# Retention of the first nine chunks in whole chunks of 128 tokens, the others in halves of 64 in quarters of the array

## The chip, the cores and the metric

The kernel runs on one core of one Trainium2 chip. The metric is the device time in microseconds (us) of one execution. Three runs of the kernel before gave 443.77, 444.45 and 444.71 us, a median of 444.45 us. A profile shows one further execution of it.

## The reference

Inputs are queries, keys and values of 4 batches, 8 heads, 768 tokens and 64 features, in float32. A retention layer with one decay per head is followed by a mixture of experts that sends each of the 3072 tokens to one of 8 experts (512 to 1024 to 512 features):

```python
gamma = 1.0 - 2.0 ** (-5.0 - np.arange(H, dtype=np.float32))
for t in range(S):
    state = gamma[None, :, None, None] * state + np.einsum('bhd,bhe->bhde', k[:, :, t], v[:, :, t])
    y[:, :, t] = scale * np.einsum('bhd,bhde->bhe', q[:, :, t], state)
...
logits = x @ w_gate + modality_bias[modality_id]
e_idx = np.argmax(logits, axis=1)
...
for e in range(E):
    mask = e_idx == e
    h = np.maximum(x[mask] @ w1[e], 0.0)
    out[mask] = gate_w[mask, None] * (h @ w2[e])
```

## The kernel before, in words

**Retention.** The 4 batches of 768 tokens are 24 chunks of 128 tokens (`NN`), six to a batch (`NCH`). The decay is taken out of the recurrence: values are scaled per token and head by a negative power of gamma on GpSimd (`decay_v`, tile `vd`), outputs by a positive power further on (`gain`). What is left for a chunk is plain matrix work in float32: scores (keys times queries, tile `sc`), a causal mask on VectorE (tile `a`), the output of a chunk (tile `y`), which is the state (tile `s`) times the queries plus the masked scores times the values, and the update of the state in PSUM (tile `st`), which ScalarE copies to SBUF (`keep_state`).

Each chunk is worked on in two halves of 64 tokens. All operands then are 64 by 64, and a matmul uses one quarter of the 128 by 128 array. `scores`, `grown` (state update) and `heads_out` (output) only make lists of matmuls; `run` issues two lists in turns of two matmuls, so that four quarters have work at once. The order within a chunk is written out in `quarters(n)`: the second half's state update and the scores of chunk n+1, in turns with the output of chunk n; then a `yield`; then the rest, with the first half's state update of chunk n+1.

**Tokens and routing.** `tokens_out` turns the output of the chunk before by a matmul with the identity and the gate's weights (tile `x`, line 308), so that it has features and logits of 128 tokens. After every third chunk `route` puts small steps on a list `todo`; the main loop takes one off at each `yield` (`tick`). They find each token's expert and its row in a DRAM tensor `x_dram` sorted by expert, and GpSimd scatters the rows there with indirect DMAs (line 414). After some groups (`EVENTS`), the first of them group 1 (chunks 3 to 5), a list of full slots of 256 rows is made: matmul `pt` (line 621), VectorE `lst` (line 625).

**Experts.** SyncE waits for that list, reads it into registers (line 879), and loads the rows (`xg`, line 735) and the weights (`raw`, lines 707 and 709). A first guess of the expert, after group 0, starts the weights earlier. Rows are transposed (`xp_e`, line 754), everything is split into a high and a low part in a reduced float32 format (ScalarE `hi`, line 713, VectorE `lo`, line 715), and the two layers are matmuls `h_e` (line 769) and `o_e` (line 784). The first job begins in the middle of chunk 9 (`DENSE`); from there on the steps of retention are put between the steps of the experts, in a fixed order. The last rows go through two static small units (`uh_u`, line 838) and a loop.

**Loads.** `load_kq` and `load_kv` put a chunk's keys and queries by feature, and its keys and values by token, on SyncE's DMA queue; SyncE works its queue off in order.

Of the kernel before, what the change touches and what calls it, by code (L numbers as in the profile page):

```python
# [7 lines left out]
F32 = mybir.dt.float32  # L8
# [26 lines left out]
NTAIL = 2  # L35
NUNIT = 144
DENSE = 9
EMPTY = 2 * NCAND
ZROW = NE * NT

# [3 lines left out]
FC = DF // P  # L44
QW = KC * 256

C_ID, C_MASK, C_DEC, C_IOTA, C_OUT, C_HALF, C_END = 0, 128, 256, 304, 312, 360, 424


@with_exitstack  # L50
def kernel(
# [23 lines left out]
    def bank(name):  # L75
        return ps.tile([P, 512], F32, tag="bank", name=name)
# [42 lines left out]

    gain = cst[:, C_OUT : C_OUT + NCH * H].rearrange("p (c h) -> p c h", h=H)  # L120
    half = cst[:, C_HALF : C_HALF + D]

    tbias = cp.tile([P, NN, NE], F32, name="tbias")
    iota3 = cp.tile([P, GRP, NE], F32, name="iota3")
# [81 lines left out]
    def masked(n):  # L206
        att[n] = wk.tile([P, 2, NG, D], F32, tag="a", name=f"a_{n}")
        nc.vector.tensor_tensor(
            att[n].rearrange("p u g t -> p (u g) t"),
            psc.pop(n).rearrange("p u g t -> p (u g) t"),  # L210
            half.unsqueeze(1).to_broadcast([P, H, D]), op=ALU.mult,
        )
# [51 lines left out]

    def quarters(n):
        more = 0 <= n and (n + 1) % NCH
        ys = []
        if n >= 0:  # L270
            py = bank(f"y_{n}").rearrange("p (g t) -> p g t", g=NG)
            ys = heads_out(n, py)
# [10 lines left out]
        if n >= 0:  # L283
            yield n
# [6 lines left out]
        if n < 0:  # L291
            return None
# [5 lines left out]
        nc.scalar.copy(yT, py)  # L298
        return yT
# [644 lines left out]

    def decay_v(n):
        vv = kvs[n][:, 1].rearrange("p (h e) -> p h e", h=H)
        vds[n] = wk.tile([P, H, D], F32, tag="vd", name=f"vd_{n}", bufs=3)
        ins = nc.gpsimd.tensor_tensor(  # L948
            vds[n], vv, dec[:, n % NCH].unsqueeze(2).to_broadcast([P, H, D]), op=ALU.mult
        )  # L950
        vd_last[:] = [getattr(ins, "ins", ins)]

# [169 lines left out]
def _layout(inputs):  # L1122
    import numpy as np

    f = np.float32
    q, k, v = inputs["q"], inputs["k"], inputs["v"]

    def feat(a):
        a = a.transpose(0, 1, 3, 2).reshape(B, NG, P, NCH, P)
        return a.transpose(0, 3, 2, 1, 4).reshape(NN, P, DM)  # L1130

    def toks(a):

        a = a.reshape(B, NG, 2, NCH, 2, D, D).transpose(0, 3, 2, 5, 4, 1, 6)
        return a.reshape(NN, P, DM)
# [7 lines left out]
    cst[:, C_DEC : C_DEC + NCH * H] = dec.reshape(P, NCH * H)  # L1143
    cst[:, C_IOTA : C_IOTA + NE] = np.arange(NE)
# [6 lines left out]
    cst[:, C_HALF:] = np.tile(np.triu(np.ones((D, D))), (2, 1))  # L1151
# [25 lines left out]
    return {n: np.ascontiguousarray(a) for n, a in arrs.items()}  # L1177
# [35 lines left out]
```

## Time and profile before

| | |
|---|---|
| median of three runs | 444.45 us (443.77 to 444.71) |
| profiled execution | 440.58 us |
| its span, first to last instruction | 438.5 us |
| TensorE (PE) busy | 402.6 us, 92% |
| VectorE (DVE) / ScalarE (ACT) / GpSimd (POOL) busy | 242.8 / 208.1 / 101.9 us |
| mean granted TensorE clock | 0.967 |
| first scores / first transposes of rows / first expert matmul | 5.26 / 64.02 / 67.38 us |

Times count from the start of the span. "PE" is matmuls, "PEld" their weight loads; a float32 matmul of the program is two instructions of each in the trace. Ends of matmuls are modelled, so the distance between starts says more than a length. A bracket behind a row gives the idle time of its engine ahead of it and what ended it; "issue" means that the engine waited for nothing the profile shows.

### The profile page before, as it was taken

Reading aid. Unit: us, or ns where it says so; the run is one execution under the profiler, and the core shown is the slowest. Engines: PE = TensorE matmul, PEld = TensorE weight load, DVE = VectorE, ACT = ScalarE, POOL = GpSimd, SP = SyncE. Lnnn points to the kernel's source line nnn. Section 1 sums busy time; section 2 is a strip of 40 time slices with the busy share of each in tenths; the row PEclk is TensorE's granted clock in tenths of the full one; section 3 lists DMA queues with packets and bytes.
Section 4 is the critical chain, followed back from the end, with each engine's and each line's share of the span. In section 5 each row is a group of like instructions: output and inputs, shape, how many; then the busy total and the mean of one; then the engine's idle time right before and its main releaser. Section 6 shows DMA issues by size and latency. Waiting matters only on the chain.

```text
span 438.5 us, 13128 instructions
## 1 busy us (share of the span) xinstructions
PE 402.6 (92%) x5156; PEld 352.2 (80%) x5156; DVE 242.8 (55%) x581; ACT 208.1 (47%) x419; POOL 101.9 (23%) x130
## 2 busy tenths in 40 slices
PE   3777788999999998999999999999999999999990
PEld 3766677878988987988888988989898898869850
DVE  1452738756656647745754765887565664635400
ACT  1331436636447555446445636645454646445310
POOL 2423312152132024021311131030486101001010
PEclk9885989999999999999999999999999999999996
DMA  8999639985967682345770224662253999995000
GB/s 287 384 386 301 218 118 305 357 271 207 323 209 243 230 314 90 116 162 178 245 277 25 76 77 165 217 194 73 92 175 117 338 343 356 332 400 222 2 24 20
DMA packets 30895, 92.83 MB, mean 212 GB/s; under 512 B 5550, under 2 KB 5678, under 8 KB 30832
## 3 DMA queue, kind: packets, MB, share of 16 engines
q1 hardware_dynamic: 25360, 77.83, 51.4%
q0 software_dynamic: 5184, 13.67, 8.3%
q8 instruction: 41, 0.67, 0.7%
q10 hardware_dynamic: 288, 0.48, 0.3%
q14 instruction: 22, 0.18, 0.1%
HBM read 94.81 MB, written 17.21 MB: 255 GB/s over the span
## 4 chain that ended last, share of the span: by engine, by line
PE 58%; issue 14%; DMA 3%; DVE 3%; ACT 2%; POOL 2%; SPq 1%; POOLq 0%; ACTq 0%
PE o_e L784 21%; PE h_e L769 21%; PE x L308 4%; PE h_s L769 3%; PE sc L263 3%; PE st L263 2%; PE y L263 2%; DVE lo_e L715 2%; DMA wa_u<-in_w_dram 2%; PE xp_e L754 1%; DMA kq<-in_qkv_dram 1%; ACT hi_e L713 1%; POOL out_dram L797 1%; DMA xg_e<-x_dram 1%; PE uh_u L838 0%
## 5 line engine op out<-in xcount | busy, mean ns | idle before, releaser
L715 DVE TENSOR_TENSOR lo_e<-raw,hi_e 128x1024 fp32r<-128x1024 f32 x80 | 99.3, 1241 | 70.1 <-ACT hi_e L713 64.9
L769 PE MATMUL h_e<-xTh,hi_e 128*128 128x256 f32 x320 | 92.2, 288 | 0.9 <-ACT hi_e L713 0.9
L769 PE MATMUL h_e<-xTh,lo_e 128*128 128x256 f32 x320 | 90.5, 283 | 0.9 <-DVE lo_e L715 0.9
L769 PE MATMUL h_e<-xTl,hi_e 128*128 128x256 f32 x320 | 90.5, 283 | 0.0
L713 ACT CAST hi_e<-raw 128x1024 fp32r<-128x1024 f32 x80 | 83.8, 1047 | 0.0
L784 PE MATMUL o_e<-hi_e,hTh 128*128 128x512 f32 x160 | 66.2, 414 | 0.0
L784 PE MATMUL o_e<-lo_e,hTh 128*128 128x512 f32 x160 | 63.3, 396 | 0.0
L784 PE MATMUL o_e<-hi_e,hTl 128*128 128x512 f32 x160 | 63.1, 394 | 0.0
L769 PEld LDWEIGHTS h_e<-xTh,hi_e 128*128 128x128 f32 x320 | 61.2, 191 | 1.9 <-ACT hi_e L713 1.1
L769 PEld LDWEIGHTS h_e<-xTh,lo_e 128*128 128x128 f32 x320 | 61.2, 191 | 1.4 <-DVE lo_e L715 1.1
L769 PEld LDWEIGHTS h_e<-xTl,hi_e 128*128 128x128 f32 x320 | 61.2, 191 | 0.0
L948 POOL TENSOR_TENSOR vd<-kv,cst 128x512 f32<-128x512 f32 x24 | 26.8, 1117 | 115.6 <-PE y L263 54.8
L722 ACT ACTIVATE hTh<-h_e 128x256 fp32r<-128x256 f32 x80 | 30.5, 387 | 35.3 <-PE h_e L769 30.0
L263 PE MATMUL sc<-kq 64*64 64x64 f32 x768 | 37.4, 239 | 9.0 <-DMA kq<-in_qkv_dram 5.3
L723 DVE SCALAR_TENSOR_TENSOR hTl<-h_e,hTh 128x256 fp32r<-128x256 f32 x80 | 33.2, 419 | 21.1 <-ACT hTh L722 19.8
L258 ACT COPY s<-st 128x256 f32<-128x256 f32 x44 | 16.5, 375 | 58.4 <-PE y L263 31.2
L797 POOL DMA_INDIRECT out_dram<-o_e,xg_e x20 | 20.7, 1035 | 92.1 <-ACT o_e L796 86.2
L263 PEld LDWEIGHTS sc<-kq 64*64 64x64 f32 x768 | 30.7, 149 | 11.0 <-DMA kq<-in_qkv_dram 5.3
L330 ACT ACTIVATE xs<-x,cst 128x64 f32<-128x64 f32 x96 | 22.2, 315 | 33.9 <-issue 24.6
L414 POOL DMA_INDIRECT x_dram<-xs,pos x24 | 25.6, 1067 | 49.2 <-DVE xs L380 22.2
L263 PE MATMUL st<-vd,kv 64*64 64x64 f32 x704 | 33.3, 240 | 3.2 <-ACT s L258 1.1
L784 PEld LDWEIGHTS o_e<-lo_e,hTh 128*128 128x128 f32 x160 | 30.1, 188 | 7.3 <-DVE lo_e L715 0.3
(181 smaller groups left out, 707.0 us busy)
## 6 DMA issues: line engine op xcount, KB each, us to landing
raw<-in_w_dram SPq DMA_DIRECT2D x104, 512.0 KB
kv<-in_qkv_dram SPq DMA_DIRECT2D x24, 512.0 KB
kq<-in_qkv_dram SPq DMA_DIRECT2D x23, 512.0 KB
xg_e<-x_dram SPq DMA_DIRECT2D x20, 257.0 KB
wa_u<-in_w_dram SPq DMA_DIRECT2D x8, 512.0 KB
wb_u<-in_w_dram SPq DMA_DIRECT2D x16, 256.0 KB
xg_s<-x_dram SPq DMA_DIRECT2D x4, 257.0 KB
x_dram<-xs,pos POOLq DMA_INDIRECT x24
```

What stands on the lines that cost most here:

```text
L263: nc.tensor.matmul(out_, l, r, start=start, stop=True, skip_group_check=True)
L308: nc.tensor.matmul(px[:, g], yT[:, 2 * u + g], wgt[:, 2 * u + g], start=(g == 0), stop=(g == 1), skip_group_check=True,)
L330: nc.scalar.activation(x[:, i], px[:, i // 2, rows(i % 2)], AF.Copy, scale=gain[:, c, 4 * u + i : 4 * u + i + 1],)
L414: ins = nc.gpsimd.indirect_dma_start(out=x_dram[:, :], out_offset=bass.IndirectOffsetOnAxis(ap=pos[:, i : i + 1], axis=0), in_=xs, in_offs ...
L713: nc.scalar.copy(hi, raws[m][i])
L715: nc.vector.tensor_tensor(lo, raws[m][i], hi.bitcast(F32), op=ALU.subtract)
L722: nc.scalar.activation(hi, src, AF.Relu)
L723: nc.vector.scalar_tensor_tensor(lo, src, 0.0, hi.bitcast(F32), op0=ALU.max, op1=ALU.subtract)
L769: nc.tensor.matmul(ph, s["w1"][f // 2][wi][:, o : o + P], s["xT"][kc // 2][a][:, kc % 2, :], start=(n == 0), stop=(n == 3 * KC - 1),)
L784: nc.tensor.matmul(po, hT[f][a][:, hh * P : (hh + 1) * P], s["w2"][f // 2][wi][:, (f % 2) * DM : (f % 2 + 1) * DM], start=(n == 0), stop=( ...
L797: ins = nc.gpsimd.indirect_dma_start(out=out[:, :], out_offset=bass.IndirectOffsetOnAxis(ap=xg.bitcast(I32)[:, DM : DM + 1], axis=0), in_= ...
L948: ins = nc.gpsimd.tensor_tensor(vds[n], vv, dec[:, n % NCH].unsqueeze(2).to_broadcast([P, H, D]), op=ALU.mult)
```

## The change

Chunks 0 to 8 (`WHOLE = 9`) are no longer halved. `whole_scores(n)` takes one head's 64 features by all 128 tokens: two heads at a time use the upper and lower half of the rows of the array, each into a PSUM bank of its own, and VectorE masks them in two operations of 512 columns where it had one. `whole_state(n)` contracts over all 128 tokens, two heads side by side in the columns, and `keep_state` copies the state once per chunk where it did twice. `whole_out(n)` does the state's part in quarters with 128 columns and the values' part over all 128 tokens. Chunks 9 to 23 keep `quarters`; `first_halves(9)` does ahead of them what the last `quarters` would have done. The masked scores of whole chunks live in the buffers of the cut weights `hi12` and `hi13`. The values' scales of whole chunks are 48 more columns of the constants, and the host lays out keys and values by token differently for these chunks.

```diff
+    def whole_scores(n):
+        kt, qt = feat(n, 0), feat(n, 1)
+        p = [bank(f"sc{j}_{n}").rearrange("p (g t) -> p g t", g=NG) for j in range(2)]
+        for g in range(NG):
+            for j in range(2):
+                nc.tensor.matmul(
+                    p[j][:, g], kt[rows(j), g], qt[rows(j), g], start=True, stop=True,
+                    skip_group_check=True,
+                )
+        att[n] = me.tile([P, 2, NG, P], F32, tag=f"hi1{2 + n % 2}", name=f"a_{n}")
+        for j in range(2):
+            nc.vector.tensor_tensor(
+                att[n][:, j], p[j], mask.unsqueeze(1).to_broadcast([P, NG, P]), op=ALU.mult
+            )
+
+    def whole_state(n):
...
+        for g in range(NG):
+            for j in range(2):
+                nc.tensor.matmul(
+                    p[rows(j), g], kk[:, 2 * g + j], vds[n][:, 2 * g + j],
+                    start=(c == 0 and g == 0), stop=True, skip_group_check=True,
+                )
+        keep_state(n + 1, 0)
...
+    def whole_out(n):
...
+                    nc.tensor.matmul(
+                        py[rows(1 - j), g], s[rows(j), g], qt[rows(j), g], start=(g == 0),
+                        stop=True, skip_group_check=True,
+                    )
+        for g in range(NG):
+            for j in range(2):
+                nc.tensor.matmul(
+                    py[rows(1 - j), g], vd[:, 2 * g + j], a[:, j, g],
+                    start=(s is None and g == 0), stop=True, skip_group_check=True,
+                )
+        yT = wk.tile([P, NG, P], F32, tag="yT", name=f"yT_{n}")
+        nc.scalar.copy(yT, py)
+        return yT
+
+    def first_halves(n):
+        run(scores(n))
+        run(grown(n, 0))
+        keep_state(n, 1)
+        masked(n)
...
     def retention(modi):
-        list(quarters(-1))
-        masked(0)
+        whole_scores(0)
...
         for n in range(NN):
-            yT = yield from quarters(n)
-            if n + 1 < NN:
-                masked(n + 1)
+            if n < WHOLE:
+                if (n + 1) % NCH:
+                    whole_state(n)
+
+                load_kv(n + 7 if n < 3 else n + 3)
+                if n + 1 < WHOLE:
+                    whole_scores(n + 1)
+                else:
+                    first_halves(n + 1)
+                yield n
+                if prev is not None:
+                    tokens_out(*prev)
+                    if n % GRP == 0:
+                        route(n // GRP - 1)
+                    prev = None
+                yT = whole_out(n)
+            else:
+                yT = yield from quarters(n)
+                if n + 1 < NN:
+                    masked(n + 1)
+                load_kv(n + 3)
             if n + 2 < NN:
                 decay_v(n + 2)
-
-            load_kv(n + 7 if n < 3 else n + 3)
             load_kq(n + 8 if n < 4 else n + 4)
```

TensorE, chunk 2, before (kq_117 are chunk 2's keys and queries, kq_125 chunk 3's; vd_250 is chunk 2's scaled values, vd_342 chunk 3's; s_2 are two copies of the state; the lines left out go on in the same turns):

```order
L308 MATMUL x_0_371<-wgt,yT_246 128x144 x2
L308 MATMUL x_1_376<-wgt,yT_246 128x144 x2
L263 MATMUL st_166<-vd_250,kv_119 64x64 x2
L263 MATMUL y_386<-kq_117,s_2_286 64x64 x2
...
L263 MATMUL sc_387<-kq_125 64x64 x2
L263 MATMUL y_386<-kq_117,s_2_336 64x64 x2
...
L263 MATMUL sc_387<-kq_125 64x64 x2
L263 MATMUL y_386<-a_340,vd_250 64x64 x2
...
L263 MATMUL st_166<-vd_342,kv_127 64x64 x2
L263 MATMUL y_386<-a_340,vd_250 64x64 x2
```

and with the change (vd_204 is chunk 2's scaled values there, and sc has two tiles):

```order
L293 MATMUL st_167<-vd_204,kv_119 64x64 x8
L275 MATMUL sc_3_318<-kq_125 128x128
L275 MATMUL sc_3_319<-kq_125 128x128
...
L366 MATMUL x_0_333<-wgt,yT_279 128x144 x2
L366 MATMUL x_1_338<-wgt,yT_279 128x144 x2
L307 MATMUL y_347<-kq_117,s_2_228 64x128 x8
L313 MATMUL y_347<-a_242,vd_204 64x128 x8
```

The turns of output with scores and state update are gone: state update, scores of the next chunk, tokens of the last, output follow each other, each in a shape of its own, with 32 matmuls in place of 64 beside the tokens' four.

SyncE's queue at the first list, before (lst_1018 is the list of group 1, xg_e_1053 the first rows; raw_109 is the last piece of the guessed weights):

```order
L707 DMA raw_109<-in_w_dram 128x1024
L102 DMA kq_618<-in_qkv_dram 128x1024
L879 TENSOR_LOAD lst_1018
L879 ISA x2
...
L735 DMA xg_e_1053<-x_dram 128x514
```

and with the change (lst_767 is that list, kv_747 are the keys and values by token of chunk 10):

```order
L765 DMA raw_109<-in_w_dram 128x1024
L104 DMA kq_474<-in_qkv_dram 128x1024
L110 DMA kv_747<-in_qkv_dram 128x1024
L937 TENSOR_LOAD lst_767
L937 ISA x2
...
L793 DMA xg_e_802<-x_dram 128x514
```

One load, that of chunk 10, has moved from behind the list to ahead of it.

More of the change, by code (lines that the diff above doesn't have):

```diff
@@ L37 @@
 DENSE = 9
+WHOLE = 9
 EMPTY = 2 * NCAND
@@ L45 @@
 QW = KC * 256
[L47 removed]
+C_ID, C_MASK, C_DEC, C_IOTA, C_OUT, C_HALF, C_DECW, C_END = 0, 128, 256, 304, 312, 360, 424, 472
 @with_exitstack
@@ L121 @@
     half = cst[:, C_HALF : C_HALF + D]
+    decw = cst[:, C_DECW : C_DECW + NCH * H].rearrange("p (c h) -> p c h", h=H)
     tbias = cp.tile([P, NN, NE], F32, name="tbias")
@@ L263, in run @@
                 nc.tensor.matmul(out_, l, r, start=start, stop=True, skip_group_check=True)
-    def quarters(n):
[L268 to L272, printed above, removed]
+    def whole_scores(n):
[12 more added lines that the diff above has]
+            )
@@ new lines, in whole_state @@
+    def whole_state(n):
+        c = n % NCH
+        if c == 0:
+            pst[n // NCH] = bank(f"st_{n}")[:, : NG * D].rearrange("p (g e) -> p g e", g=NG)
+        p = pst[n // NCH]
+        kk = kvs[n][:, 0].rearrange("p (h d) -> p h d", h=H)
+        for g in range(NG):
[5 more added lines that the diff above has]
+        keep_state(n + 1, 0)
+        if c == NCH - 2 and n + 1 < WHOLE:
+            pst.pop(n // NCH)
@@ new lines, in whole_out @@
+    def whole_out(n):
+        py = bank(f"y_{n}").rearrange("p (g t) -> p g t", g=NG)
+        qt, a, vd, s = feat(n, 1), att.pop(n), vds.pop(n), sts.pop((n, 0), None)
+        if s is not None:
+            for g in range(NG):
[4 more added lines that the diff above has]
+                    )
+        for g in range(NG):
+            for j in range(2):
+                nc.tensor.matmul(
[5 more added lines that the diff above has]
+        return yT
@@ L273, in quarters @@
+    def first_halves(n):
[3 more added lines that the diff above has]
+        masked(n)
+    def quarters(n):
+        more = (n + 1) % NCH
+        py = bank(f"y_{n}").rearrange("p (g t) -> p g t", g=NG)
+        ys = heads_out(n, py)
         own = grown(n, 1) if more else []
@@ L946, in decay_v @@
         vv = kvs[n][:, 1].rearrange("p (h e) -> p h e", h=H)
+        by = decw if n < WHOLE else dec
         vds[n] = wk.tile([P, H, D], F32, tag="vd", name=f"vd_{n}", bufs=3)
         ins = nc.gpsimd.tensor_tensor(
-            vds[n], vv, dec[:, n % NCH].unsqueeze(2).to_broadcast([P, H, D]), op=ALU.mult
+            vds[n], vv, by[:, n % NCH].unsqueeze(2).to_broadcast([P, H, D]), op=ALU.mult
         )
@@ L1130, in feat, with whole @@
         return a.transpose(0, 3, 2, 1, 4).reshape(NN, P, DM)
+    def whole(a):
+        return a.transpose(0, 2, 1, 3).reshape(NN, P, DM)[:WHOLE]
     def toks(a):
+        w = whole(a)
         a = a.reshape(B, NG, 2, NCH, 2, D, D).transpose(0, 3, 2, 5, 4, 1, 6)
-        return a.reshape(NN, P, DM)
+        return np.concatenate([w, a.reshape(NN, P, DM)[WHOLE:]])
     gam = 1.0 - 2.0 ** (-5.0 - np.arange(H, dtype=np.float64))
@@ L1143, in _layout @@
     cst[:, C_DEC : C_DEC + NCH * H] = dec.reshape(P, NCH * H)
+    dec = (gam[None, :] ** (-t[:, None])).reshape(NCH, P, H)
+    cst[:, C_DECW:] = dec.transpose(1, 0, 2).reshape(P, NCH * H)
     cst[:, C_IOTA : C_IOTA + NE] = np.arange(NE)
@@ L1150, in _layout @@
     cst[:, C_OUT : C_OUT + NCH * H] = gain.transpose(1, 0, 2).reshape(P, NCH * H)
-    cst[:, C_HALF:] = np.tile(np.triu(np.ones((D, D))), (2, 1))
+    cst[:, C_HALF : C_HALF + D] = np.tile(np.triu(np.ones((D, D))), (2, 1))
     ci = np.arange(NCAND)
```

5 lines of the change are left out of this document (1 added, 4 removed).

## The prediction

> **What bounds the kernel now.** I read the page first, then busy time by stretch, then the order of single instructions around the first list of rows.
>
> ```profile
> PE   3777788999999998999999999999999999999990
> PEclk9885989999999999999999999999999999999996
> ...
> 8.30:64.00 55.70, 43.92 (x1201) 39.10 (x1202) 24.84 (x109) 17.76 (x57) 17.24 (x30) 0.82 0.83 294
> 68.60:421.00 352.40, 347.37 (x3826) 305.18 (x3827) 213.77 (x466) 183.00 (x350) 80.31 (x91) 1.00 0.60 207
> ```
>
> The second pair gives, per stretch, its length, busy PE, PEld, DVE, ACT and POOL, granted clock, DMA share and GB/s. From 68.6 to 421 us TensorE is busy 347.37 of 352.40 us at full clock: the expert matmuls, in one fixed order. The change leaves that stretch alone, so the end moves by as much as its start moves. Before it lies a head of 55.70 us, in which the first nine chunks run by themselves; there PE idles 11.8 us and the clock averages 0.82. By stretch:
>
> ```profile
> 8.30:13.40 5.10, 4.62 (x128) 4.43 (x128) 1.01 (x5) 0.74 (x2) 3.05 (x11) 1.00 1.06 367
> 13.40:16.80 3.40, 1.56 (x82) 1.27 (x82) 2.02 (x10) 1.23 (x3) 0.55 (x2) 1.00 1.02 405
> 16.80:20.20 3.40, 3.40 (x73) 3.28 (x64) 1.72 (x10) 0.86 (x2) 1.89 (x2) 0.50 1.03 406
> 20.20:30.50 10.30, 6.88 (x248) 6.16 (x250) 5.02 (x23) 4.38 (x17) 1.38 (x6) 1.00 1.03 389
> 30.50:44.10 13.60, 11.34 (x268) 9.84 (x261) 4.32 (x20) 3.02 (x9) 5.25 (x6) 0.50 0.94 302
> 44.10:57.80 13.70, 9.92 (x292) 8.38 (x288) 8.17 (x39) 4.61 (x15) 5.13 (x6) 1.00 0.62 221
> 57.80:61.20 3.40, 3.40 (x57) 3.00 (x51) 1.59 (x6) 1.04 (x3) 0.00 (x0) 0.50 0.09 22
> ```
>
> and, as single instructions (start, length, instruction):
>
> ```profile
> 10.17 0.32 PE L263 MATMUL st<-vd,kv 64*64 64x64 f32 x2
> 10.18 0.32 PE L263 MATMUL y<-kq,s 64*64 64x64 f32 x2
> 10.27 0.32 PE L263 MATMUL st<-vd,kv 64*64 64x64 f32 x2
> ...
> 14.25 0.23 PE L263 MATMUL st<-vd,kv 64*64 64x64 f32 x2
> 14.26 0.23 PE L263 MATMUL y<-kq,s 64*64 64x64 f32 x2
> 14.31 0.23 PE L263 MATMUL st<-vd,kv 64*64 64x64 f32 x2
> ```
>
> Three stretches are at 0.50. The first one is too, though the profile gives it 1.00: four quarter instructions start every 0.10 us at 10.2 and every 0.06 us (0.058 over longer runs) at 14.3. The clock falls after a stretch that PE spent half idle (1.56 of 3.40 busy before 16.8) and rises after a full one. Half clock covers 4.62 + 3.40 + 11.34 + 3.40 = 22.8 us of busy time, so about 11.4 us are lost to it. The idle time has this form:
>
> ```profile
> 16.55 0.27 PE L263 MATMUL y<-kq,s 64*64 64x64 f32 x1 [1.37 <-issue]
> 34.22 0.37 PE L263 MATMUL y<-kq,s 64*64 64x64 f32 x2 [1.07 <-issue]
> ...
> q8 instruction: 41, 0.67, 0.7%
> ```
>
> PE waited for nothing the profile shows. PE ran 10,312 matmuls and loads; 0.67 MB for them is 64 bytes each, and 41 packets is 16 KB, 256 instructions, each. A chunk of quarters is 128 matmuls and 128 loads: one packet per chunk. I read those gaps as PE running out of instructions (a guess: the view only names them "issue").
>
> **The change, part by part.** Per chunk it replaces 64 quarter matmuls by 32 (each is two instructions in the trace), run two at a time in place of four. Prices:
>
> ```profile
> 379.77 1.93 PE L838 MATMUL uh_u<-wa_u,uxT_u 128*32 128x256 f32 x32
> 381.64 0.39 PE L769 MATMUL h_s<-xTh,hi_s 128*128 128x256 f32 x1
> 62.93 1.25 PE L308 MATMUL x<-wgt,yT 128*128 128x144 f32 x8
> 64.02 1.34 PE L754 MATMUL xp_e<-cst,xg_e 128*128 128x128 f32 x8
> 119.84 0.28 PE L769 MATMUL h_e<-xTh,lo_e 128*128 128x256 f32 x1
> 119.96 0.28 PE L769 MATMUL h_e<-xTl,hi_e 128*128 128x256 f32 x1
> 120.17 0.27 PE L263 MATMUL st<-vd,kv 64*64 64x64 f32 x2
> ```
>
> The tail unit runs four column tiles over all 128 rows: 32 instructions of 256 columns in 1.87 us, 0.058 us each. Each tile thus gets a new one every 0.23 us. Half the columns on half as many tiles at once give the same pitch, so a pair with 128 columns starts every 0.058 us, one with 64 columns every 0.029. So whole scores cost 16 x 0.058 = 0.93 us, the state's part of the output 0.93, the values' part 0.93, the state update 0.46: 3.25 us, against 128 x 0.058 / 4 = 1.86. The token matmuls (8 in 1.09 us, from 62.93 to 64.02) stay. Going from one shape of the array to another costs 0.09 us (119.96 to 120.17 is 0.21, where the pitch is 0.12); whole chunks do it four times, quarters twice. A chunk is thus 3.13 us before and 4.70 now, **1.6 us more at full clock**; over the head, 12 to 13 us more.
>
> The Trainium skill, TensorEngine Tiling (Array Packing), Tiling Modes, says that a change of tiling mode drains the array. By the trace that drain is 0.09 us; if it took a whole instruction, 0.27 us, the 18 extra changes would cost 3.2 us more, and the forecast below would be about 2 us faster than before instead of 5.
>
> What pays for it is time in which PE now does nothing or runs at half clock. I lay out the new order from 8.30 us, where the first state update starts as before (values scaled on POOL wait for the constants, which grow by a ninth). The rows that pin it:
>
> ```profile
> 7.21 1.04 POOL L948 TENSOR_TENSOR vd<-kv,cst 128x512 f32<-128x512 f32 x1 [6.12 <-DMA cst<-in_consts_dram]
> 44.89 2.23 PE L308 MATMUL x<-wgt,yT 128*128 128x144 f32 x16
> 45.06 0.59 ACT L298 COPY yT<-y 128x512 f32<-128x512 f32 x1
> 49.66 0.20 PE L548 MATMUL pc<-ones,crep 128*96 128x1 bf16 x1 [0.84 <-DVE crep L543]
> 51.18 0.40 PE L570 MATMUL pk<-dg,onef 96*96 96x96 f32 x2
> 54.09 0.21 PE L621 MATMUL pt<-ohs,vals 96*1 96x2 bf16 x3 [0.18 <-DVE ohs L611]
> 57.44 0.15 DVE L625 TENSOR_TENSOR lst<-pt,base_e 1x6 int32<-1x6 f32 x1 [3.40 <-remote]
> 60.03 1.67 SPq L735 DMA_DIRECT2D xg_e<-x_dram  x2
> L208 DVE TENSOR_TENSOR a<-sc,cst 128x512 f32<-128x512 f32 x9 | 6.2, 685 | 16.9 <-PE sc L263 12.8 <-PE y L263 4.1
> ```
>
> At half clock: state 0 to 9.4, scores 1 to 11.4, output 0 to 13.3. That fills the stretch, so the clock rises at 13.4 as it does now, and full prices hold from there. Chunk 1 ends at 18.0, chunk 2 at 22.7. Its copy (0.59 and 0.2 of hand-over) and token matmuls end at 24.7. State 3 and scores 4 end at 26.3; then PE waits for the first group's routing on DVE, 2.5 us behind the token matmuls (47.12 to 49.66 today), until 27.5 with its small matmul. Chunk 3 ends at 29.9, chunk 4 at 34.6, chunk 5 with its copy and tokens at 40.8. Scores 7 end at 42.4, the counts (pc) wait until 43.3, output 6 (no state) ends at 44.8, pk at 45.1. From pk to pt it is 2.9 us on DVE (51.18 to 54.09), and 0.7 more for the second mask, as a chunk now has two of 0.685 us: pt at 48.4 in place of 54.09. From there PE has token matmuls 6 and 7, outputs 7 and 8, state 8 and the first halves of chunk 9, 8.5 us, to the first transposes xp_e: 56.9 in place of 64.02.
>
> The other way to xp_e is the list: DVE waited 3.40 us after pt, and xp_e came 6.6 us after lst. If both stay, xp_e is at 48.4 + 3.6 + 6.6 = 58.6, so the list, not PE, sets it. I take 59: some issue gaps will remain, but with half the instructions in a chunk, one packet lasts nearly two chunks. **The head is 5 us shorter.** Bounds: 11.8 us of idle and 11.4 us of clock are all there is to win, against 12.7 us of added work, so at best 10 to 11 us net; at worst all the idle time stays, and only 11.4 less about 2.5 (the cold start) is won against 12.7: 4 us slower.
>
> Edits costed at nothing: the one state copy less per chunk (0.37 us on ACT, covered by ACT's 17.76 busy of 55.70); the second mask (DVE busy 24.84, plus 6.2; the mask has the length of a token step and an output to be done in, and if not covered costs 0.7 per chunk); the masks' home in the cut weights' buffers, free since output 8 is issued ahead of the first cut of those. The load of chunk 10's keys and values now stands ahead of the list on SP. It waits for state 7, which PE issues before pt, so it delays nothing; the row reads behind it share the engines with 0.5 MB, 1.7 us at 302 GB/s at the very most.
>
> **Rivals.** *The pairs do not overlap in the scores* (slower). Each scores instruction loads 128 columns, as the token matmuls do, and those follow each other at 0.136 us. If two row halves do not run together, scores cost 16 x 0.136 = 2.18 us, 1.25 more, in eight chunks 10 us: the head is 5 us longer, 449.5. It decides from a pitch above about 0.10. Against it: the quarter rows at 14.25, where both row halves write the same partitions and still start within 0.06 us of each other. The same holds for pairs that share all rows: the Trainium skill, TensorE: Matmul & The Clock Gate, Part 3, says that weight loads overlap running matmuls only where the row groups differ. By that rule state update and values' part would double, 1.4 us a chunk, 12 us, 451; uh_u, four tiles on the same rows at 0.058, speaks against it. *The clock stays low* (slower): if 22.8 us of busy time are at half clock again, 9 us of the clock's gain are gone, and the head is 4 us longer, 448.5; for it speaks the stretch from 30.5 to 44.1, cold for 13.6 us with PE busy 11.34; against it, that longer instructions leave fewer holes. *Something else starts the experts* (no change): the guessed weights, scatters and row reads set xp_e, or the later stages swallow the gain; against it, PE is full until 62 and the row reads hang on pt. *All holes go*: xp_e near 53, 11 us less, 433.5.
>
> **Numbers.** The profiled execution took 440.58 us with a span of 438.5; the median of the runs shown is 444.45. 5 us less is 435.6 of the first and **439.5** of the second. Chances: forecast (2 to 9 us less) 0.65; all holes go 0.12; no change 0.08; pairs 0.10 (scores 0.07, rows 0.03); clock 0.05. Faster by over 0.2% (0.9 us, about what can be told here) 0.77, same 0.08, slower 0.15. The range goes from 433.5 to 445.5, and leaves the slower cases out. The forecast's own is 435.5 to 442.5.
>
> **What would show it.** Right: starts of scores, state and values' parts 0.05 to 0.07 us apart at full clock (0.03 for the state update); clock 1.00 from about 13.4 on with at most one cold stretch; issue gaps before 35 us cut to a third; pt near 50 and xp_e near 59; the time from the first h_e to the end unchanged within 2 us. Wrong: a pitch of 0.1 or more, cold stretches of more than 10 us, xp_e at 63 or later, or a tail that gives the head's gain back.

## The result and the profile after

| | before | after |
|---|---|---|
| median, same series | 444.58 us (443.77 to 445.04, 4 runs) | 436.67 us (435.64 to 437.91, 4 runs) |
| ratio | | 0.9832 [0.9800, 0.9863] |
| profiled execution, and its span | 440.58 us, 438.5 us | 436.40 us, 434.3 us |
| its mean granted clock | 0.967 | 0.982 |
| counts (pc), slot keys (pk), list matmul (pt) start | 49.66, 51.18, 54.09 us | 44.38, 47.57, 51.17 us |
| first transposes (xp_e) start | 64.02 us | 60.72 us |

The changed kernel is 7.9 us faster by the medians and 4.2 us by the two profiled executions: the profiled execution of the kernel before was quicker than any of those four runs.

The page of the kernel after has these rows (busy tenths and granted clock in 40 slices, and the queue that brings instructions):

```profile
PE   4988789999999998999999999999999999999990
PEclk9999699999999999999999999999999999999995
q8 instruction: 36, 0.59, 0.5%
```

Its busy time by stretch (length, PE, PEld, DVE, ACT, POOL, granted clock, DMA share, GB/s):

```profile
8.40:60.70 52.30, 46.69 (x641) 40.64 (x641) 30.80 (x120) 15.27 (x51) 18.51 (x31) 0.93 0.89 321
...
65.40:417.80 352.40, 347.99 (x3830) 305.34 (x3830) 213.34 (x466) 183.77 (x350) 78.70 (x91) 1.00 0.60 206
```

In the second stretch PE is as busy as before (347.99 us, and 347.37 before). Its length of 352.40 us was chosen alike in both kernels and shows nothing; the starts of instructions do. From the first `h_e` to `uf_u` of the last unit it was 67.38 to 422.15 us before, and is 64.15 to 417.95 us now: 354.8 and 353.8 us (354.5 and 354.0 in the repetitions below). So 3.2 of the 4.2 us are won ahead of the first expert matmul, and about 1 us behind it. In the head PE is idle for 52.30 - 46.69 = 5.6 us, where it was 11.8, and runs 641 matmuls at a clock of 0.93, where it ran 1201 at 0.82.

What PE waited for in the head of the kernel before (total us, times, longest):

```profile
PE y L263 <- issue: 5.6, 8, 1.5
PE sc L263 <- issue: 3.0, 4, 1.9
...
PE st L263 <- issue: 1.0, 2, 0.7
```

and in that of the kernel after:

```profile
PE x L366 <- ACT yT L318: 2.5, 3, 1.1
PE pk L628 <- DVE rkt L455: 1.6, 1, 1.6
PE st L293 <- POOL vd L1007: 0.9, 1, 0.9
PE pc L606 <- DVE crep L601: 0.8, 1, 0.8
PE totg L642 <- DVE cnt L429: 0.6, 1, 0.6
```

All 9.6 us of "issue" are gone. The largest new wait, 1.6 us, is pk's, and VectorE is behind it. Single instructions of VectorE and GpSimd in the kernel after (start, length, instruction, and in brackets the idle time before it with its releaser):

```profile
44.24 1.28 DVE L281 TENSOR_TENSOR a<-sc,cst 128x512 f32<-128x512 f32 x2
45.44 0.20 DVE L611 TENSOR_SCALAR size<-pc,cnd 96x1 f32<-96x1 f32 x1
...
46.07 1.04 POOL L1007 TENSOR_TENSOR vd<-kv,cst 128x512 f32<-128x512 f32 x1 [5.07 <-issue]
...
46.12 1.00 DVE L620 TENSOR_TENSOR key<-key,first_g 96x1 f32<-96x1 f32 x1
...
51.27 1.29 DVE L281 TENSOR_TENSOR a<-sc,cst 128x512 f32<-128x512 f32 x2 [2.06 <-PE sc L275]
52.48 0.14 DVE L683 TENSOR_TENSOR lst<-pt,base_e 1x6 int32<-1x6 f32 x1
```

Two masks, 1.28 us together, stand between the counts and the slots' sizes, then `key`, one number in each of 96 partitions, takes 1.00 us while GpSimd multiplies, and two more masks stand ahead of the list. The same step among VectorE's instructions of the kernel before took 0.15 us:

```profile
50.58 0.15 DVE L562 TENSOR_TENSOR key<-key,first_g 96x1 f32<-96x1 f32 x1
```

And the chain of work of the kernel after, to the first run of expert matmuls:

```profile
44.33 1.20 DVE a L281 x2
...
46.12 1.02 DVE key L620
...
51.62 5.42 DMA x_dram<-xs,pos
57.06 0.36 SPq L793
...
57.63 3.83 DMA xg_e<-x_dram
61.50 0.56 PE xp_e L812 x3
...
65.41 1.59 PE h_e L827 x11
```

From 44 to 61 us the chain is not on PE: masks, `key`, the scatter of the tokens' rows (5.42 us to land) and the read of the first rows. PE reached its own transposes at about the same time. What the read waited for last was not the list: `lst` was made at 52.48 us, SyncE was through with it at about 55.2, and then waited for the scatter.

```profile
SPq L793 <- DMA x_dram<-xs,pos: 1.8, 1, 1.8
```

### The profile page after: what moved, and what is told of

Its sections match the earlier page's. It is cut to its first block, busy times and chain, and to the rows that moved or that the text cites. A ratio compares the mean times of both kernels' runs of the same rounds, so it can differ in the third digit from the quotient of the medians.

```text
span 434.3 us, 11970 instructions
## 1 busy us (share of the span) xinstructions
PE 405.2 (93%) x4580; PEld 353.3 (81%) x4580; DVE 247.6 (57%) x590; ACT 205.5 (47%) x410; POOL 101.4 (23%) x130
## 4 chain that ended last, share of the span: by engine, by line
PE 72%; issue 9%; DMA 7%; DVE 5%; ACT 3%; POOL 2%; SPq 1%; POOLq 0%; ACTq 0%
PE h_e L827 24%; PE o_e L842 23%; PE x L366 5%; PE h_s L827 3%; PE sc L266 3%; PE st L266 2%; PE y L266 2%; PE xp_e L812 2%; PE sc L275 2%; DMA wb_u<-in_w_dram 2%; DVE lo_e L773 2%; PE y L313 2%; DMA xg_e<-x_dram 2%; DMA cst<-in_consts_dram 1%; DMA x_dram<-xs,pos 1%
## 5 line engine op out<-in xcount | busy, mean ns | idle before, releaser
L773 DVE TENSOR_TENSOR lo_e<-raw,hi_e 128x1024 fp32r<-128x1024 f32 x80 | 98.1, 1226 | 68.9 <-ACT hi_e L771 63.1
L827 PEld LDWEIGHTS h_e<-xTh,hi_e 128*128 128x128 f32 x320 | 60.8, 190 | 1.6 <-ACT hi_e L771 0.7
L827 PEld LDWEIGHTS h_e<-xTh,lo_e 128*128 128x128 f32 x320 | 60.7, 190 | 1.4 <-DVE lo_e L773 1.1
L827 PEld LDWEIGHTS h_e<-xTl,hi_e 128*128 128x128 f32 x320 | 60.8, 190 | 0.0
L781 DVE SCALAR_TENSOR_TENSOR hTl<-h_e,hTh 128x256 fp32r<-128x256 f32 x80 | 33.3, 420 | 20.5 <-ACT hTh L780 19.3
L388 ACT ACTIVATE xs<-x,cst 128x64 f32<-128x64 f32 x96 | 22.3, 315 | 42.5 <-issue 19.3
L842 PEld LDWEIGHTS o_e<-hi_e,hTh 128*128 128x128 f32 x160 | 30.1, 188 | 5.9
L842 PEld LDWEIGHTS o_e<-hi_e,hTl 128*128 128x128 f32 x160 | 30.2, 189 | 5.4
L366 PE MATMUL x<-wgt,yT 128*128 128x144 f32 x192 | 31.3, 306 | 2.6 <-ACT yT L318 2.5
L854 ACT ACTIVATE o_e<-o_e,xg_e 128x512 f32<-128x512 f32 x20 | 13.8, 691 | 40.0 <-issue 25.5
```

What stands on the lines that cost most here:

```text
L366: nc.tensor.matmul(px[:, g], yT[:, 2 * u + g], wgt[:, 2 * u + g], start=(g == 0), stop=(g == 1), skip_group_check=True,)
L388: nc.scalar.activation(x[:, i], px[:, i // 2, rows(i % 2)], AF.Copy, scale=gain[:, c, 4 * u + i : 4 * u + i + 1],)
L773: nc.vector.tensor_tensor(lo, raws[m][i], hi.bitcast(F32), op=ALU.subtract)
L781: nc.vector.scalar_tensor_tensor(lo, src, 0.0, hi.bitcast(F32), op0=ALU.max, op1=ALU.subtract)
L827: nc.tensor.matmul(ph, s["w1"][f // 2][wi][:, o : o + P], s["xT"][kc // 2][a][:, kc % 2, :], start=(n == 0), stop=(n == 3 * KC - 1),)
L842: nc.tensor.matmul(po, hT[f][a][:, hh * P : (hh + 1) * P], s["w2"][f // 2][wi][:, (f % 2) * DM : (f % 2 + 1) * DM], start=(n == 0), stop=( ...
```

## The experiments

### How far the kernel before wanders

Both kernels were timed again, unchanged, in two later series on two chips.

> The kernel before, unchanged, beside itself, so that it has spans and clocks of several executions. The one profiled so far took 440.58 us, the timed ones 443.8 to 445.0. Both theories expect no difference from the kernel before. If the clock's cold stretches fall differently from run to run, the spans should differ by some us and go with the mean clock: 438.5 us came with 0.967, so 441.5 to 443 should come with 0.955 to 0.965.

> The changed kernel unchanged, so that it stands beside the others of this series: 436 to 437, spans within 2 us of each other, as its clock hardly varies (0.982 to 0.986 so far).

The kernel before against itself: 442.74 us (440.69 to 445.52, 10 runs) against 443.55 (439.29 to 449.10, 25 runs), ratio 1.0005 [0.9966, 1.0044]. Without three runs of 446 us and more, the time of the other 32 goes with the mean granted clock, 0.959 to 0.977: 1.8 us less for each 0.01 (correlation -0.55). The 11 runs below 0.966 have a median of 444.00 us, the 15 at 0.970 and above 441.68. The kernel after again: 437.37 (436.72 to 438.62, 4 runs) against 443.17, ratio 0.9871 [0.9779, 0.9963], with the same wait of 1.6 us at pk and the same stretch at half clock (46.6 to 53.5 us). So the gain is real, and the clock of the kernel after varies less: 0.982 to 0.986 in its eight runs.

In the table that the rest is read from, "issue" is PE's time in such gaps up to the first transposes, "half clock" counts from 13.5 us up to there; all from profiled executions, one for each row. Three whole chunks, six, and masks late have 3.4 us more at half clock 4 to 6 us behind the start of xp_e, which the table leaves out.

| kernel | issue, us | half clock, us | pt | xp_e |
|---|---|---|---|---|
| before | 9.6 | 20.5 | 54.1 | 64.0 |
| before, again | 11.4 | 13.7 | 54.6 | 64.3 |
| before, load early | 10.0 | 17.1 | 56.4 | 66.5 |
| 3 whole chunks | 4.0 | 17.1 | 50.8 | 61.4 |
| 6 whole chunks | 1.7 | 10.2 | 49.5 | 59.9 |
| after (9 whole) | 0 | 6.8 | 51.2 | 60.7 |
| after, again | 0.2 | 6.8 | 51.1 | 60.8 |
| after, load late | 0.2 | 0 | 49.3 | 58.7 |
| after, masks late | 0 | 3.4 | 49.8 | 59.9 |
| after, both late | 0 | 0 | 48.6 | 57.2 |

### Three and six whole chunks

```diff
-WHOLE = 9
+WHOLE = 3      (and = 6 in the second kernel)
```

> Only the first three chunks whole. Theory A (the gain is the idle time of PE named issue, plus half-clock time, less more array work): the two longest holes lie in these chunks (1.37 and 1.50 us, the third at 27.3 us follows), so a third to a half of the 7.9 us: 440 to 442. Theory B (the gain comes from the load of chunk 10 being ahead of the list): nothing, 444.5, since that load is behind the list again here.

> The first six chunks whole. Theory A: most of the gain, 437 to 439.5; chunks 6 to 8 still have the holes of quarters around the list. Theory B: nothing, 444.5, as the load of chunk 10 is behind the list.

Three: 438.95 us (436.56 to 441.90, 10 runs), ratio 0.9919 [0.9875, 0.9963]. Six: 435.63 (434.62 to 438.04, 5 runs), 0.9827 [0.9759, 0.9894]. With three, PE's waits in the head are:

```profile
PE y L266 <- issue: 2.9, 4, 2.1
PE pc L606 <- DVE crep L601: 1.5, 1, 1.5
PE totg L642 <- DVE cnt L429: 1.2, 1, 1.2
PE pt L679 <- DVE ohs L669: 1.2, 1, 1.2
PE st L266 <- issue: 1.1, 2, 0.7
```

Both are faster than expected (440 to 442, and 437 to 439.5). The gaps that are left stand at the lines of the halves (L266). They go from 9.6 us over 4.0 and 1.7 to nothing with each three chunks that become whole, and about half of the gain comes with the first three. That half is not the clock's: ten runs with three whole chunks have 0.963 to 0.979, as the kernel before; with six it is 0.977 to 0.983. The last three chunks bring nothing that can be told: by then the gaps are nearly gone, and PE's waits for routing on VectorE (pc, totg and pt, 1.2 to 1.5 us each with three whole chunks already) are what is left ahead of the list.

### The moved load

The change also moved the load of chunk 10's keys and values ahead of the list on SyncE's queue. Once it was moved alone in the kernel before, and once put back in the kernel after:

```diff
 (before)                                 (after)
+            load_kv(n + 7 if ...)   |  -                load_kv(n + 7 if ...)
             yield n                 |   ...
 ...                                 |               decay_v(n + 2)
-            load_kv(n + 7 if ...)   |  +            load_kv(n + 7 if ...)
```

> The kernel before with one part of the change alone: the load of keys and values by token is issued ahead of the step that makes the list, quarters as before. Theory A: no change (within 1 us of 444.5). Theory B: the whole gain, 437.

> The changed kernel with the load of keys and values by token back behind the step that makes the list. Theory A (idle time named issue and half-clock time are gone, for more array work): no change, 436.5 within 1 us, and in the trace chunk 10's load behind the list again. Theory B (the moved load): back to 443.5. After the third run B is unlikely, this is its counterpart.

Alone: 443.65 us (441.39 to 445.43, 10 runs), ratio 1.0008 [0.9972, 1.0044]. Put back: 436.51 (435.58 to 438.45, 4 runs), 0.9855 [0.9758, 0.9951], beside 0.9871 of the kernel after in the same series. The load has no part in the gain, and six whole chunks had all of it with that load behind the list. In the one profile with the load behind the list xp_e starts at 58.7 us and waits 1.0 us for its rows; that head has no stretch at half clock, so the 2 us are not put down to the load. In the one profile with the load moved alone xp_e starts at 66.5 us, but `pt` was 1.8 to 2.3 us late there already; only 1.2 to 1.4 us more pass from the list to the read of the rows than before. So a cost of about 1 us is neither shown nor excluded.

### PE kept busy, instructions as before

The kernel before with four matmuls of 512 columns, whose sums nothing reads, ahead of each step of retention (76 in all, 72 of them ahead of the transposes):

```diff
+    def fill():
+        p = bank("fill")
+        for _ in range(4):
+            nc.tensor.matmul(p, ones, fillr, start=True, stop=True)
...
         for n in ret:
+            fill()
             tick()
```

> The kernel before, with 4 matmuls of ones by ones, 512 columns in bf16, added at each of the 18 steps of the head, whose result nobody reads: 72 of 0.21 us, 15.4 us of array work at full clock, about what whole chunks add, but with all the instructions of quarters. Theory A1 (the clock follows the array's load, and it is the clock that pays): half-clock time falls from about 23 to under 10 us of busy time, holes shrink because each step lasts longer, and the time stays at 442 to 446. Theory A2 (the number of instructions pays, the clock comes with it): holes named issue stay near 9 us, cold stretches stay, and the time goes up by 8 to 15 us, to 452 to 459.

447.78 us (445.79 to 450.90, 10 runs), ratio 1.0117 [1.0078, 1.0157]: slower by 5.2 us for 15.4 us of array work added ahead of the transposes. Its head, and PE's waits there:

```profile
8.40:66.00 57.60, 51.35 (x1263) 36.59 (x1264) 25.70 (x108) 17.20 (x56) 17.31 (x30) 1.00 0.79 285
```

```profile
PE y L265 <- issue: 3.4, 6, 1.2
...
PE rk L388 <- issue: 0.7, 1, 0.7
PE st L265 <- issue: 0.7, 2, 0.4
```

With PE busier the clock stays at 1.00 from 14.7 us to the end of the head, though nothing else was changed, and all ten runs have a mean clock of 0.980 to 0.990, where the kernel before had at most 0.977: the half clock of the kernel before follows from PE's idle time. (This profile has 6.8 us at half clock much later, from 339 us on, and is slower than its median.) So 10 us of the 15 come back. The gaps fall only to about 5 us. The time lies between the ranges of both theories (442 to 446, and 452 to 459): the clock is as the first one has it, the gaps half as the second. A fuller PE keeps the clock up, but does not close the gaps.

### Masks behind the routing step

```diff
     def whole_scores(n):
 ...
+        psc[n] = p
+
+    def whole_masked(n):
+        p = psc.pop(n)
         att[n] = me.tile(...)
 ...
                 yield n
+                if n + 1 < WHOLE:
+                    whole_masked(n + 1)
```

> The changed kernel with the two masks of a chunk put behind the routing step on VectorE in place of ahead of it; nothing else moves. If the masks, costed at nothing in the prediction, hold up the list (TensorE waited 1.65 us for pk, and the clock fell to half right behind it), pk comes 1.3 to 1.7 us earlier, the cold stretch from 46.5 us goes, and the time is 1.5 to 4 us less: 432.5 to 435. If the rows' way to DRAM and back sets the first expert matmul anyway, under 1 us is won.

435.63 us (434.39 to 436.41, 4 runs), ratio 0.9813 [0.9721, 0.9905], 1.7 us below the kernel after of the same series. PE's order there:

```profile
46.08 0.38 PE L632 MATMUL pk<-dg,onef 96*96 96x96 f32 x2
46.39 0.69 PE L297 MATMUL st<-vd,kv 128*64 128x64 f32 x16
47.01 1.16 PE L275 MATMUL sc<-kq 64*128 64x128 f32 x16
49.75 0.21 PE L683 MATMUL pt<-ohs,vals 96*1 96x2 bf16 x3 [1.58 <-DVE ohs L673]
```

pk comes 1.5 us earlier and no longer waits. The wait moves on to pt (1.58 us), because another small VectorE step now runs beside GpSimd's multiplication, and the two masks stand behind it, still ahead of pt's own steps:

```profile
46.36 0.94 DVE L439 TENSOR_SCALAR den<-den 128x3 f32<-128x3 f32 x1
...
47.54 1.27 DVE L285 TENSOR_TENSOR a<-sc,cst 128x512 f32<-128x512 f32 x2
```

pt is 1.4 us earlier. So the masks and the slow small step are on the chain, as the profile after says, and the masks' place alone cost the list 1.4 us. What that is worth in time is less clear. The forecast here, 432.5 to 435 us without a stretch at half clock, was missed: 3.4 us of it are left from 50.5 us on, 3.4 more follow from 64.1 us on, in the first expert matmuls, and the profiled execution took 436.41 us, as long as the kernel after's 436.40 and 436.72. Only the medians of four runs each differ.

### The guessed weights left out

The kernel before without the early load of the guessed expert's weights; the weights come when the list is known:

```diff
-                raw(guess, 1)
-                raw(guess, 2)
...
-                    raw(job, 1, guess)
-                    raw(job, 2, guess)
+                    raw(job, 1)
+                    raw(job, 2)
```

> The kernel before without the weights of the guessed expert (4 MB from 32 us on); they come after the list instead, so the first expert matmul is some 10 us later and the whole slower; read here are only the holes between 33 and 44 us. Theory F (PE's instructions come late because their packets stand behind data in the DMA engines): the hole of 1.07 us at 33 us and the four small ones from 35.8 to 38.3 us (1.1 us together) go. Theory S (the scatters of GpSimd hold PE's instructions up, whatever the rest of the traffic): the small ones stay, 0.25 to 0.4 us each, as in the stretch from 53.9 to 57.4 us, where the traffic was low.

442.65 us in one run, beside 438.31 (434.65 to 440.54, 11 runs) of the kernel before on this chip; the first expert now waits for weights and rows, and is not the question here. The stretch from 32 to 46 us is, first in the kernel before, then without the guess:

```profile
32.00:46.00 14.00, 11.76 (x257) 10.47 (x258) 4.03 (x18) 3.58 (x10) 5.91 (x7) 0.57 0.92 282
```

```profile
32.00:46.00 14.00, 10.88 (x398) 9.79 (x397) 8.50 (x39) 6.41 (x21) 6.44 (x8) 1.00 0.35 125
```

By their times the two profiles are of different chips. With the transfers at 0.35 in place of 0.92 the same 14 us take 398 matmuls in place of 257, but the clock is 1.00 there in place of 0.57 too, so that the counts alone tell little. The five gaps of the kernel before (1.07, 0.29, 0.26, 0.35, 0.24 us) become two (0.64 and 1.11), and the four small ones from 55 to 57.4 us are gone. The packets of 16 KB on the instruction queue come 3.6 to 4.4 us apart there; in the kernel before, up to 50 us, never less than 5.1 us apart (4.8 in its repetition), also at full clock and with PE waiting (5.1 and 6.2 us between 20.5 and 31.8 us). So instructions reached PE faster where the data queues were quiet. Theory S falls, since the small gaps went though the scatters stayed; theory F holds in part only, since one long gap stayed (1.07 to 0.64 us) and one of 1.11 us is new. The gaps before 24 us, ahead of the guessed weights, did not shrink (1.95 and 3.39 us, against 1.37 and 1.50, or 1.62 and 3.11 in the repetition).

### As many instructions as before, in whole chunks

The kernel after with 32 matmuls of eight columns ahead of each step, in pairs of quarters, so that the head has 1218 matmuls again:

```diff
+    def fill():
+        p = bank("fill")
+        for i in range(32):
+            r = c = rows(i % 2)
+            nc.tensor.matmul(
+                p[c, 0:8], ones[r, 0:D], fillr[r, 0:8], start=(i < 2), stop=True, ...
```

> The changed kernel, with 18 bursts of 32 matmuls of eight columns in pairs of quarters, whose sums nothing reads, one burst ahead of each step of the recurrence's stretch: 576 more TensorE instructions of almost no work, so that the head holds about as many (641 + 576) as before the change (1201). Nothing else is changed, and no transfer is added. By the pitch of 0.03 us of a quarter in the kernel before at full clock, the bursts are worth 17 us of TensorE's time by themselves. Theory N (the holes called issue are TensorE running out of instructions that have to be fetched, so they follow the number of instructions): the holes come back, 4 to 10 us of issue waits in the head, and the time is 436.7 + 17 + 4 to 10, that is 458 to 464. Theory K (the holes belong to the quarters' own form, with its two row halves and four places, not to the count): no issue waits above 1 us, and 450 to 456. The verdict goes by the issue waits, since the price of such a small matmul is not known from any row.

449.06 us (two runs of 443.31 and 446.56, two near 452) beside 444.94 (440.55 to 448.05, 7 runs). The profiled execution took 446.56 us, with xp_e at 71.4: 10.7 us later than after, about the price of 18 bursts (0.60 us for 32, at full clock), where the expectation had put 17. PE's waits up to there are:

```profile
PE x L368 <- ACT yT L320: 1.5, 2, 0.7
PE st L295 <- POOL vd L1009: 0.9, 1, 0.9
PE y L309 <- issue: 0.6, 2, 0.3
PE y L315 <- issue: 0.2, 1, 0.2
```

0.8 us of "issue" where the theory that counts instructions wanted 4 to 10: it falls as it was put. Bursts of 0.019 us per matmul, faster than any quarter, run without a gap of over 0.3 us, and as many packets of instructions are fetched as before the change (41 in the whole program). What this kernel does not match is the need per time: 1218 matmuls in 63.0 us, one packet in 6.6 us on average, while the halves of the kernel before, without gaps, need one in 3.1 us at full clock (256 instructions in a chunk). The two readings that are left, a supply that cannot hold one packet in 3 us beside the transfers, and something in the quarters' own form, were not told apart by a run.

The traces tell them apart for the long gaps. Counted over all of PE's instructions in the trace, these stand, in the kernel before, exactly 256 instructions or twice that from each other, which is one packet, and each ends 1.1 to 1.5 us after a packet has landed:

| gap, us | 1.37 | 1.50 | 1.93 | 1.07 | 0.29 | 0.69 |
|---|---|---|---|---|---|---|
| its end, us | 16.55 | 23.02 | 29.21 | 34.22 | 47.89 | 53.09 |
| PE's instructions ahead of it | 449 | 705 | 961 | 1217 | 1729 | 1985 |
| last packet landed, us | 15.29 | 21.92 | 27.80 | 32.82 | 46.55 | 51.58 |

In the repetition, with the load early, with the filled PE, without the guess and with three whole chunks, too, every gap of "issue" of more than 0.45 us ahead of the transposes stands at one of these counts, or at 1473; in the filled PE the one at 1217 is ahead of a routing matmul of 128 by 128 (`rk` above), not of a quarter. So in the long gaps PE has run out of instructions, and waits for the next packet. They make 6.9 of the 9.6 us. The short ones (0.2 to 0.4 us, 0.7 to 0.8 us from one to the next) stand at no such count, and their cause stays open, as does what makes a packet late.

### Masks late and fewer whole chunks, masks late and the load late

Two candidates for a better kernel, both with the masks behind the routing step: one with `WHOLE = 6`, one with nine whole chunks and the load behind the list again.

> Six whole chunks, with the masks behind the routing step. If the holes that are left for chunks 6 to 8 (1.7 us with six whole chunks) and their cold stretch cost about what the quarters save in array work (3 x 1.6 us), the time is that of nine: 435.6 within 1 us. If the masks hold up the list here as well, 1 to 2 us below six whole chunks alone: 434.

> Nine whole chunks, masks behind the routing step and the load of keys and values by token behind the list. The load took nothing in the fifth run, so no change against masks late alone: 435.6 within 1 us. If its 0.5 MB hold up the scatters' landing or the rows, which are the chain's next steps (5.4 and 3.8 us), up to 1 us less.

Six chunks: 432.53 us (429.47 to 433.65, 6 runs), ratio 0.9861 [0.9813, 0.9909]; its profile has 0.5 us of issue waits and half clock from 57.6 to 67.8 us. Nine, with the load late: **429.82 us (429.10 to 431.68, 6 runs), ratio 0.9827 [0.9783, 0.9870]**, against 438.31 on the same chip, which is some 5 us faster than the others, so that only ratios carry over. By its ratio the second is 435.5 where the kernel before takes 443.17, as expected if the load does nothing. In both the load of chunk 10 stands behind the list, so they differ in the number of whole chunks and in the place of earlier loads; their 2.7 us are not clear of noise, since the ratios overlap. Head and dense stretch of the second:

```profile
8.40:57.20 48.80, 44.32 (x641) 38.57 (x641) 30.55 (x120) 15.26 (x51) 17.32 (x30) 1.00 0.92 333
60.60:413.00 352.40, 348.25 (x3838) 305.49 (x3839) 214.36 (x467) 185.79 (x353) 80.93 (x93) 1.00 0.60 210
```

The clock holds at 1.00 from 13.0 us to the end of the dense stretch, and the transposes start at 57.2 us, 6.8 earlier than in the profile before. This is the best profile of the study, and the kernel beats the one before. Part of its lead is probably the chip's: from the first `h_e` to `uf_u` it takes 350.4 us, where the kernels before and after took 353.8 to 354.8 on theirs. Whether it beats the kernel after is not settled: that one was not run in this series, and the ratios (0.9827 against 0.9832 and 0.9871) overlap.

## Why the prediction was right, and where it was off

Forecast 439.5 us, measured 436.67. Sign and mechanism held: array time is paid, gaps and half clock go. Two sizes were off, and they partly cancelled, so that the closeness of the number is in part luck.

**The dense stretch is only shifted.** Right within the 2 us that the forecast allowed: from the first `h_e` to the end 371.1 us before and 370.1 after.

**The prices of the parts.** Right. PE's order in the kernel after, at full clock:

```profile
16.64 1.09 PE L313 MATMUL y<-a,vd 128*64 128x128 f32 x16
17.57 0.63 PE L293 MATMUL st<-vd,kv 128*64 128x64 f32 x16
18.13 1.16 PE L275 MATMUL sc<-kq 64*128 64x128 f32 x16
19.22 1.25 PE L366 MATMUL x<-wgt,yT 128*128 128x144 f32 x8
20.40 1.09 PE L307 MATMUL y<-kq,s 64*64 64x128 f32 x16
21.42 1.09 PE L313 MATMUL y<-a,vd 128*64 128x128 f32 x16
```

From start to start a values' part takes 0.93 us, a state update 0.56, scores 1.09, tokens 1.18, the state's part 1.02: 4.78 us a chunk, where 4.70 was forecast with its four changes of shape. The scores take 0.068 us each, changes of shape included, far below the 0.10 from which the rival decides. So **pairs do not overlap** falls in both forms: the update and the values' part, whose pairs share all rows, run at 0.035 and 0.058. By the Trainium skill (TensorE: Matmul & The Clock Gate, Part 3) the shared rows should have kept weight loads from overlapping; the trace does not agree.

**The clock rises at 13.4 and stays.** Nearly: it rises at 12.3 and has one cold stretch, 46.5 to 53.3 us, that was not in the forecast's schedule. **The clock stays low** falls. That PE's idle time brings the half clock is shown best by the filled PE; with whole chunks the clock rises too, but only from six on. The kernel after, with no gaps left, still has one such stretch, behind its wait for pk.

**The issue gaps.** Forecast cut to a third before 35 us; they vanished. The guess on their cause, PE running out of instructions, holds for the long gaps, which stand at the borders of packets, and stays open for the short ones. Their number alone is not what counts, since an equal number in another mix did not bring the gaps back; that it is the number per time is argued from the packets, not shown by a run.

**The schedule.** Forecast and measured start, us:

| step | forecast | measured |
|---|---|---|
| tokens of chunk 2 done | 24.7 | 24.4 |
| chunk 5 with its tokens done | 40.8 | 41.8 |
| pc | 43.3 | 44.38 |
| pk | 45.1 | 47.57 |
| pt | 48.4 | 51.17 |
| xp_e | 59 | 60.72 |

Up to pc it holds to about 1 us. **The step that failed is the second mask's cover: "0.7 more for the second mask, as a chunk now has two", between pk and pt alone, and "the second mask" among the edits costed at nothing.** Two masks come at once, 1.28 us, and they stand ahead of the slots' sizes, so pk already is late; `key` adds 0.85 us by meeting GpSimd. The masks made late bring pk back by 1.5 us. From pk to pt the sum fits by luck: 3.6 us were put (2.9 and 0.7 for a mask; its own 48.4 for pt is 0.3 short of them), and 3.6 were measured, but no mask was in them. VectorE had pt's operand ready at 49.20 us, and PE came to pt only at 51.17, behind state update and scores at half clock; with that clock at 1.00 (load late) pk to pt took 2.0 us. The forecast also said that the list, not PE, sets xp_e. It was neither alone: the list was ready, and SyncE waited 1.8 us more for the scatter to land, which the forecast had not named. From pt to xp_e it took 9.55 us where 10.2 were put, but in other parts: 1.3 to the list and 8.2 from there, where 3.6 and 6.6 were put.

**From the profile to the median.** The forecast took the same 5 us off both. The two profiles differ by 4.2 us (forecast 5, the slipped routing explains the lack), but the medians by 7.9. This step was mis-sized: the profiled run of the kernel before was a quick one, 4.0 us below its median, and that of the kernel after only 0.3 below. The kernel before loses about 1.8 us for each 0.01 of clock and its runs spread over 0.959 to 0.977, while the kernel after has 0.982 to 0.986 in all eight; that the median gains what this spread cost is an argument from these numbers, not an experiment. In the other series the medians differ by 5.8 us.

**Something else starts the experts** falls, since the head moved and the end with it. **All holes go** came true of the holes, but not of its time (433.5), since the routing took over; masks and load late reach xp_e at 57.2, still behind the 53 of that rival. The load of chunk 10 costed at nothing was right within what the medians can tell.

## What to carry to other kernels

A form of work that needs twice the instructions can lose more by gaps, and by the half clock that follows them, than its better packing wins: look at PE's "issue" waits and the granted clock by stretch before counting array time. When such gaps close, ask which small chain on another engine comes next; here two masks put ahead of a routing step cost the list 1.4 us that their order alone gives back. To learn what an unnamed gap is, count the engine's instructions up to it: gaps at a fixed count are a matter of supply. And compare a kernel that loses its clock by medians over many runs, since one profile of it may be a quick one.

## What the runs showed of the hardware

- **Clock.** All stretches between two changes of the clock are multiples of 3.413 us (3.4, 6.8, 10.2, 13.7). The clock fell after a window with PE far from idle, 43.1 to 46.5 us of the kernel after:

```profile
43.10:46.50 3.40, 1.99 (x31) 1.48 (x28) 3.12 (x12) 0.92 (x3) 0.43 (x1) 1.00 1.02 416
```

  and did not fall after an emptier one of the best kernel, 47.1 to 50.5 us:

```profile
47.10:50.50 3.40, 1.85 (x21) 1.67 (x23) 2.99 (x12) 0.00 (x0) 2.70 (x3) 1.00 0.66 254
```

  Busy time in a window alone does not tell whether the clock falls; what does was not found. Ahead of the first change the profile gives 1.00, though the pitch of the matmuls is that of half clock. In the kernel with tiny matmuls the first rise came as late as 22.3 us.
- **PE's instructions** come in packets of 256. In the halves' kernel its gaps of more than 0.45 us that wait for nothing shown stand at whole numbers of packets and end 1.1 to 1.7 us after one has landed.
- **Small VectorE steps beside GpSimd.** `key` on 96 partitions by 1 took 1.00 us in place of 0.15 while GpSimd multiplied 128 by 512, and ended with it. The Trainium skill (SBUF — State Buffer, Who interferes with whom) says that a VectorE step with two inputs in SBUF and a GpSimd step that reads SBUF block each other wholly: the one issued second waits until the first is done. The trace agrees: `key` started at 46.12, within GpSimd's 46.07 to 47.11, and ended at 47.12.
- **Tiny matmuls.** Pairs of quarters with eight columns started every 0.019 us (32 in 0.60 us) at full clock.
